# Retention attention feeding a gated MLP: tables on ScalarE's queue, the mask moved up, attention blocks set further apart

## The chip, the cores and the metric

The kernel runs on one core of one Trainium2 chip, in one launch. The metric is the device time of that launch in microseconds (us); the times shown are medians. The core's engines run side by side, each with its own list of instructions in a fixed order: TensorE (PE in the profile, its weight loads PEld), VectorE (DVE), ScalarE (ACT), GpSimd (POOL) and SyncE (SP), which only starts transfers here. They wait for each other by semaphores.

## The reference, cut to what matters

```python
# attention: batch 4, heads 8, seq 768, head_dim 64
gamma = 1.0 - 2.0 ** (-5.0 - np.arange(H))
for t in range(S):
    state = gamma * state + k_t v_t^T          # one 64x64 state per batch and head
    y[:, :, t] = (q_t @ state) / sqrt(D)
x = y.transpose(0, 2, 1, 3).reshape(B, S, H * D)   # 4 x 768 x 512
# MLP
gate = sigmoid(causal conv of x over time, 5 taps, per channel)
val = x @ w_val                                 # 512 x 512
out = (gate * val) @ w_out                      # 512 x 512
```

All inputs are float32; the weights and `conv_w` come as float64 words and are turned into float32 on the chip.

## The kernel before, in words

**Tiles.** The sequence is cut into 6 chunks of 128 tokens. An attention block `g` (0 to 23) is chunk `c = g // 4` of batch `b = g % 4`, all 8 heads. A chunk that is whole (4 blocks) gives `x` for the MLP: 4 `val` tiles (channels) and then 4 `out` tiles (batches), each of 12 matmuls of 128x512, because each product is made of three float32r matmuls (`xh`, `xl` are the rounded part of x and the rest; `wvh`, `wvl`, `woh`, `wol` those of the weights; `gvh`, `gvl` those of gate times val). 48 tiles in all; the last one is done in two halves.

**An attention block.** One 1 MB load `att` brings q, k, v, k (block 0 in two halves, q and k first); POOL scales v by a decay table (`decay`, L249). PE makes scores (`sy<-att`, L259). DVE masks them (`mask`, L269, writes `u`). Then PE does y from the masked scores (`y_scores`, `sy<-u,att`, L297) and the state update of the first half (`z_ps`, L281); both together are `block_a`. `block_b` is the second state update, y from the state that ACT copied (`snap`, L292), and from block 6 on the scores of the next block. DVE evacuates y into `x` (`evac`, L342). In PE's instructions each of the small products is a weight load and a matmul, done twice for float32: a block has 112 to 128 such pairs, a `val` or `out` tile 12.

**Beside it.** Each of the 8 weight pieces (512 KB, `wst`) is converted by five DVE steps, one of ACT and one of POOL (L386 to L415), and then split (L426, L430); `cw_raw`, the conv weights, takes the same path with 20 columns. For each `val` tile ACT does the first conv tap and DVE the other four (`tap`, L443; PE may take one or two instead), ACT the sigmoid, and DVE multiplies gate and val (`gated`, L478).

**What sets the order.** Every piece of work is a step, made by `at(due, engine, cost, reads, writes, ...)`. `plan` sorts the steps by `due`, and then walks through a modelled time: whenever an engine is free, it takes the ready step with the lowest `due`. The result is the fixed order of each engine's instructions. Costs and due times have no other effect. `LATE_STEP` spaces the due times of attention blocks 6 to 23 and `MLP_STEP` those of the tiles. In the model PE also waits for its instructions: after every `PAGE` pairs the next page is there `FETCH` us after the page before the last one ended.

**Transfers.** `get` loads the small tables: `small_sb` (decay, ratio and mask), `cw_raw`, `pos_sb`, `eye_sb`. All transfers start from SP, in the order of its list; each takes one of eight semaphores in turn, and the transfer that takes it again waits until the one before has landed. PE multiplies `pos_sb` into a base table (`first_pos`, L322) ahead of the first `y_scores`.

Of the kernel before, what the change touches and what calls it, by code (L numbers as in the profile page):

```python
# [27 lines left out]
LATENCY, LANDING = 0.15, 1.8  # L28
PAGE, FETCH = 128, 4.0
TINY = 2.0 ** -15 * (1.0 + 1.0 / 8.0)  # L30
# [10 lines left out]
class Step:  # L41
    def __init__(self, due, engine, cost, reads, writes, fn, args):
        self.due, self.engine, self.cost, self.fn, self.args = due, engine, cost, fn, args
        self.reads, self.writes = reads, writes
        self.waits, self.then = set(), []
        self.next = []
        self.after = []
        self.ready = 0.0
        self.words = 0
        self.other = None  # L50


def plan(steps):
# [39 lines left out]
    clock, free = {}, {}  # L93
# [11 lines left out]
    while any(free.values()):  # L105
# [11 lines left out]
        if e == "PE" and s.words:  # L117

            left, now = s.words, start
            while left >= words:  # L120
                now += s.cost * words / s.words
                left -= words
                paged.append(now)
                now, words = max(now, paged[-2] + FETCH), PAGE
            words -= left
# [7 lines left out]
        for t in s.then:  # L133
            late = LANDING if e == "DMA" else 0.0 if t.engine == e else LATENCY
            t.ready = max(t.ready, clock[e] + late)
            t.waits.discard(s.index)
# [7 lines left out]
def tile_retention_gated_mlp(  # L144
# [91 lines left out]
    def get(dst, src):  # L236
        nc.sync.dma_start(out=dst, in_=src)

# [293 lines left out]
    MM = 0.232  # L532
    EARLY_AT = 2.6
    EARLY_STEP = 2.8
    LATE_AT = 28.7
    LATE_STEP = 3.05
    MLP_AT = 31.2
    MLP_STEP = 10.2
    SPLIT_LEAD = 5.4
    CONV_LEAD = 6.1  # L540
    W_AT = (9.3, 15.6, 15.6, 22.7, 32.7, 35.7, 38.7, 41.7)

    loaded = {}

    def load_at(due, g):
        loaded[g] = due
        a = [("att", g % LB, "qk"), ("att", g % LB, "vk")]
        if g == 0:
            at(due, "DMA", 1.4, [], a[0:1], load, g, slice(0, 2))
            at(due, "DMA", 0.2, [], ["small"], get, small_sb, small)  # L550
            at(due, "DMA", 1.4, [], a[1:2], load, g, slice(2, 4))
            at(due, "DMA", 0.1, [], ["cwraw"], get, cw_raw,
               conv_w.bitcast(I32).rearrange("p (n two) -> p n two", two=2))
            at(due, "DMA", 0.1, [], ["pos"], get, pos_sb, pos)
        else:
            at(due, "DMA", 2.6, [], a, load, g)
# [11 lines left out]

    scored, summed = {}, {}

    def attention(g, t, ahead):
# [34 lines left out]
        if b == 0:  # L606
            xbufs[c] = Slot("x", XB)
            last = [xbufs[c - 1]] + [("x", c - 1, i) for i in range(B)] if c else []
            at(t + 3.5, "ACT" if c else "DVE", 0.25, last,
               [xbufs[c]] + [("x", c, i) for i in range(B)], new_x, c)  # L610
        at(t + 5.0, "DVE", 0.62, [y, ("dec", c % 2), xbufs[c]], [("x", c, b)], evac, g)
        if g + LB < NG:
# [82 lines left out]
    for i in range(WARM):  # L695
        at(0, "PE", 0.43, [], [Slot("acc", 2) if i < 2 else "sy1"], warm_up, i)
    at(0, "ACT", 1.5, [], ["table"], first_sigmoid)
    load_at(0, 0)
    for due, w, n in ((0.1, 1, 0), (0.2, 0, 1), (0.3, 1, 1), (0.4, 0, 2), (0.5, 1, 2), (0.6, 0, 3), (0.7, 1, 3), (0.8, 0, 4)):
        if w or n < LB:  # L700
            (load_w_at if w else load_at)(due, n)
        if due == 0.3:
            at(due, "DMA", 0.2, [], ["eye"], get, eye_sb, eye)
    at(5.05, "PE", 1.0, ["pos", ("att", 0, "vk")], ["sy1"], first_pos)
    at(5.06, "ACT", 0.6, ["sy1"], ["base", ("dec", 0)], base_copy)
    convert(4.0, "cw")
    for m in range(NPAIR):
# [117 lines left out]
```

## Time and profile before

| | |
|---|---|
| Median of 3 runs | 234.3 us (234.22 to 234.41) |
| Profiled execution, time | 235.24 us |
| Profiled execution, span from first to last instruction | 233.5 us |
| PE, DVE, ACT, POOL busy | 209.3, 140.2, 105.7, 105.7 us |
| Instructions of PE | 3549 weight loads, 3549 matmuls |

The profile comes from one execution, which was 0.9 us above the median; the time holds 1.7 us more than the span. Busy time of PE counts a matmul from its start to its modelled end, and matmuls overlap, so rate is read from the distance between starts.

### The profile page before, as it was taken

The page shows a single profiled execution, that of the slowest core. Times are in us where ns is not written, and L with a number is a line of the kernel's source. Part 1 is how long each engine was busy: PE and PEld are TensorE (multiplying, and loading weights), DVE is VectorE, ACT ScalarE, POOL GpSimd, SP SyncE. Part 2 cuts the span into 40 slices and gives each one's busy share as a digit, 9 for nine tenths or more (in the row PEclk, how much of TensorE's full clock was granted, in tenths as well). Part 3 has the DMA queues.
Part 4 walks back from the last instruction along what each step waited for, and adds up shares of the span by engine and source line. Part 5 has one row for each costly group of instructions (what it writes and reads, how often), then busy time and mean ns, then how long its engine had stood idle before and what let it go on. Part 6 is the DMA issues. An engine that isn't in the chain of part 4 may idle for free.

```text
span 233.5 us, 7952 instructions
## 1 busy us (share of the span) xinstructions
PE 209.3 (90%) x3549; PEld 163.5 (70%) x3549; DVE 140.2 (60%) x213; ACT 105.7 (45%) x218; POOL 105.7 (45%) x93
## 2 busy tenths in 40 slices
PE   8276666998799998897998999999999999999994
PEld 3166655766577776675776778888888888888884
DVE  0488678999999998322296636169617861921100
ACT  2363285238855842243544322664376426521322
POOL 0257879677996281116822020582078208220400
PEclk9975697999999999998899999999999999999999
DMA  5999979963565665545250101111111111111122
GB/s 155 381 428 413 380 276 345 414 234 117 181 219 206 243 239 199 206 173 215 65 213 3 48 4 49 45 46 45 48 45 45 45 47 63 59 58 45 45 93 90
DMA packets 8822, 36.32 MB, mean 156 GB/s; under 512 B 1106, under 2 KB 1618, under 8 KB 5844
## 3 DMA queue, kind: packets, MB, share of 16 engines
q1 hardware_dynamic: 8788, 35.82, 41.0%
q8 instruction: 28, 0.46, 0.8%
q14 instruction: 6, 0.05, 0.1%
HBM read 29.52 MB, written 6.29 MB: 153 GB/s over the span
## 4 chain that ended last, share of the span: by engine, by line
PE 61%; DVE 19%; issue 7%; POOL 5%; ACT 3%; DMA 3%; SPq 0%; POOLq 0%; ACTq 0%; DVEq 0%
PE mm L497 27%; PE mm L469 22%; DVE acc L443 9%; PE sy L297 6%; PE sy L259 3%; DMA att<-in_att_dram 3%; PE z_ps L281 3%; DVE x L342 3%; DVE u L269 2%; POOL rest L411 2%; POOL att L249 2%; DVE gate L478 1%; ACT xh L351 1%; DVE rest L415 1%; POOL wvl L430 1%
## 5 line engine op out<-in xcount | busy, mean ns | idle before, releaser
L443 DVE SCALAR_TENSOR_TENSOR acc<-x,cw_sb,acc 128x512 f32<-128x512 f32 x95 | 70.5, 753 | 17.2 <-ACT acc L441 15.1
L489 POOL TENSOR_TENSOR gvl<-gate,gvh 128x512 fp32r<-128x512 f32 x24 | 30.8, 1291 | 44.6 <-ACT gvh L485 34.4
L355 POOL TENSOR_TENSOR xl<-x,xh 128x512 fp32r<-128x512 f32 x24 | 30.5, 1284 | 31.8 <-PE mm L469 28.5
L497 PE MATMUL mm<-woh,gvh 128*128 128x512 f32 (+1 forms) x100 | 39.4, 394 | 0.0
L497 PE MATMUL mm<-wol,gvh 128*128 128x512 f32 (+1 forms) x100 | 39.3, 393 | 0.0
L497 PE MATMUL mm<-woh,gvl 128*128 128x512 f32 (+1 forms) x100 | 39.3, 393 | 0.0
L249 POOL TENSOR_TENSOR att<-att,small_sb 128x512 f32<-128x512 f32 x24 | 25.1, 1044 | 29.1 <-DMA att<-in_att_dram 27.3
L507 ACT COPY o_sb<-mm 128x512 f32<-128x512 f32 (+1 forms) x25 | 14.3, 571 | 37.0 <-PE mm L497 36.9
L269 DVE TENSOR_TENSOR u<-sy,small_sb 128x512 f32<-128x512 f32 x24 | 16.5, 686 | 24.0 <-PE sy L259 24.0
L478 DVE TENSOR_TENSOR gate<-mm,gate 128x512 f32<-128x512 f32 x24 | 16.4, 685 | 22.2 <-PE mm L469 22.2
L469 PE MATMUL mm<-xl,wvh 128*128 128x512 f32 x96 | 28.5, 407 | 0.0
L469 PE MATMUL mm<-xh,wvh 128*128 128x512 f32 x96 | 28.2, 410 | 0.0
L469 PE MATMUL mm<-xh,wvl 128*128 128x512 f32 x96 | 28.1, 404 | 0.0
L485 ACT CAST gvh<-gate 128x512 fp32r<-128x512 f32 x24 | 14.9, 620 | 26.2 <-DVE gate L478 17.6
L297 PEld LDWEIGHTS sy<-u,att 64*64 64x64 f32 x768 | 16.0, 152 | 14.4 <-issue 5.8
L259 PE MATMUL sy<-att 64*64 64x64 f32 x768 | 18.8, 232 | 7.4 <-issue 6.3
L297 PE MATMUL sy<-u,att 64*64 64x64 f32 x768 | 19.1, 243 | 5.9 <-DVE x L342 3.6
L281 PE MATMUL z_ps<-att 64*64 64x64 f32 x704 | 22.1, 240 | 2.3 <-issue 1.0
L292 ACT COPY snap<-z_ps 128x256 f32<-128x256 f32 x44 | 14.5, 371 | 19.0 <-PE z_ps L281 19.0
L281 PEld LDWEIGHTS z_ps<-att 64*64 64x64 f32 x704 | 17.3, 150 | 8.1 <-ACT snap L292 5.2
L259 PEld LDWEIGHTS sy<-att 64*64 64x64 f32 x768 | 15.9, 147 | 9.0 <-issue 7.0
L497 PEld LDWEIGHTS mm<-woh,gvh 128*128 128x128 f32 x100 | 18.9, 189 | 4.2
(46 smaller groups left out, 264.6 us busy)
## 6 DMA issues: line engine op xcount, KB each, us to landing
att<-in_att_dram SPq DMA_DIRECT2D x23, 1024.0 KB, 5.8
out_dram<-o_sb SPq DMA_DIRECT2D x23, 256.0 KB, 2.0
wst<-in_w_dram SPq DMA_DIRECT2D x8, 512.0 KB, 7.2
att<-in_att_dram SPq DMA_DIRECT2D x2, 512.0 KB, 5.5
out_dram<-o_sb SPq DMA_DIRECT2D x2, 128.0 KB, 1.7
small_sb<-in_small_dram SPq DMA_DIRECT2D x1, 68.0 KB, 4.1
eye_sb<-in_eye_dram SPq DMA_DIRECT2D x1, 64.0 KB, 8.5
cw_raw<-in_conv_w_dram SPq DMA_DIRECT2D x1, 20.0 KB, 6.4
```

Source lines behind the costliest of these rows:

```text
L249: nc.gpsimd.tensor_tensor(v, v, vd_sb[:, c, :].unsqueeze(2).broadcast_to([P, 8, HALF]), op=ALU.mult)
L259: nc.tensor.matmul(sy[cols, x, (2 * j + s) * HALF:(2 * j + s + 1) * HALF], lhsT=kT[rows, x, j, s, :], rhs=q[rows, x, j, s, :], start=True, ...
L269: nc.vector.tensor_tensor(us[g], sy[:, :, 0:256].rearrange("p x (a t) -> p x a t", t=HALF), tri_sb.unsqueeze(1).unsqueeze(1).broadcast_to( ...
L281: nc.tensor.matmul(z_ps[cols, x, b, j], lhsT=k[rows, x, j, s, :], rhs=v[rows, x, j, s, :], start=g == 0 and s == 0 and j == 0, stop=True, ...
L297: nc.tensor.matmul(sy_of(g)[cols, h, off:off + HALF], lhsT=lhsT, rhs=rhs, start=start, stop=True, skip_group_check=True,)
L355: nc.gpsimd.tensor_tensor(xl[n, ct], xs[n][:, ct, :, HALO:], xh[n, ct].bitcast(F32), op=ALU.subtract)
L443: nc.vector.scalar_tensor_tensor(acc, x[:, :, k:k + P], cw_sb[:, m, k:k + 1], acc, op0=ALU.mult, op1=ALU.add,)
L469: nc.tensor.matmul(vps[n, m], lhsT=w[:, m, ct * P:(ct + 1) * P], rhs=xx[n, ct].rearrange("p b t -> p (b t)"), start=(i == 0), stop=(i == 3 ...
L478: nc.vector.tensor_tensor(gv, vps.pop((n, m)), gv, op=ALU.mult)
L485: nc.scalar.copy(gvs[n, m][0], gate[n, m])
L489: nc.gpsimd.tensor_tensor(gvl, gate.pop((n, m)), gvh.bitcast(F32), op=ALU.subtract)
L497: nc.tensor.matmul(ops[n, b, cs.start][:, 0:cs.stop - cs.start], lhsT=gg[:, b * P:(b + 1) * P], rhs=w[:, ct, cs], start=(i == 0), stop=(i ...
```

## The change

Four things are changed. The small tables are loaded by ScalarE's queue, ahead of its table load, and no longer lie between SP's transfers; `first_pos` no longer waits for the second half of block 0. In the planner the page wait has two lengths (3.4 us, or 5.0 while transfers are under way, in place of 4.0). The costs and due times of the start are others: the conversion of `cw_raw` is due at 9.0 and not at 4.0. And due times are spaced otherwise: 6.0 for attention blocks in place of 3.05, 3.6 for tiles in place of 10.2, where a `val` tile is never due before its chunk is whole (`whole`). The work itself is the same.

```diff
-PAGE, FETCH = 128, 4.0
+PAGE, FETCH, CROWDED = 128, 3.4, 5.0
...
+        self.lag = 0.0
...
-                now, words = max(now, paged[-2] + FETCH), PAGE
+                slow = clock.get("DMA", 0.0) > now
+                now, words = max(now, paged[-2] + (CROWDED if slow else FETCH)), PAGE
...
-            t.ready = max(t.ready, clock[e] + late)
+            t.ready = max(t.ready, clock[e] + late + s.lag)
...
     def get(dst, src):
-        nc.sync.dma_start(out=dst, in_=src)
+        nc.scalar.dma_start(out=dst, in_=src)
...
-    LATE_STEP = 3.05
-    MLP_STEP = 10.2
+    LATE_STEP = 6.0
+    MLP_STEP = 3.6
...
         if g == 0:
-            at(due, "DMA", 1.4, [], a[0:1], load, g, slice(0, 2))
-            at(due, "DMA", 0.2, [], ["small"], get, small_sb, small)
-            at(due, "DMA", 1.4, [], a[1:2], load, g, slice(2, 4))
-            at(due, "DMA", 0.1, [], ["cwraw"], get, cw_raw,
+            at(due, "DMA", 3.2, [], a[0:1], load, g, slice(0, 2))
+            at(due, "DMA", 1.6, [], a[1:2], load, g, slice(2, 4))
+            at(due, "ACT", 0.4, [], ["small"], get, small_sb, small)
+            at(due, "ACT", 0.4, [], ["pos"], get, pos_sb, pos)
+            at(due, "ACT", 0.4, [], ["cwraw"], get, cw_raw,
                conv_w.bitcast(I32).rearrange("p (n two) -> p n two", two=2))
-            at(due, "DMA", 0.1, [], ["pos"], get, pos_sb, pos)
+            at(due, "ACT", 0.4, [], ["eye"], get, eye_sb, eye)
+            for s in steps[-4:]:
+                s.lag = 5.0
...
+        whole[c] = t + 5.1
...
-    at(0, "ACT", 1.5, [], ["table"], first_sigmoid)
     load_at(0, 0)
+    at(0.05, "ACT", 1.5, [], ["table"], first_sigmoid)
...
-        if due == 0.3:
-            at(due, "DMA", 0.2, [], ["eye"], get, eye_sb, eye)
-    at(5.05, "PE", 1.0, ["pos", ("att", 0, "vk")], ["sy1"], first_pos)
+    at(5.05, "PE", 1.0, ["pos"], ["sy1"], first_pos)
...
-    convert(4.0, "cw")
+    convert(9.0, "cw")
...
+    t = MLP_AT - MLP_STEP
     for p, (what, n, m) in enumerate(order):
-        t = MLP_AT + MLP_STEP * p
+        t += MLP_STEP
+        if what is val_tile:
+            t = max(t, whole[n] + max(SPLIT_LEAD, CONV_LEAD))
```

Lines from L44 on have numbers higher by one to seven in the changed file; the text below uses those of the kernel before, the rows of the changed order their own.

What this does to the order is shown at three places. First DVE, from its first instruction that waits for a transfer. `u<-sy,small_sb` is the mask of block 0, 128x20 are the conversion steps of `cw_raw`, `wst` is the first weight piece. Before:

```order
L386 TENSOR_SCALAR acc<-cw_raw 128x20
L392 SCALAR_TENSOR_TENSOR top<-cw_raw,acc 128x20
L398 TENSOR_SCALAR acc<-top 128x20
L402 SCALAR_TENSOR_TENSOR rest<-cw_raw,acc 128x20
L415 SCALAR_TENSOR_TENSOR cw_sb<-acc,rest 128x20
L386 TENSOR_SCALAR acc<-wst 128x512
L269 TENSOR_TENSOR u<-sy,small_sb 128x512
```

And now:

```order
L388 TENSOR_SCALAR acc<-cw_raw 128x20
L394 SCALAR_TENSOR_TENSOR top<-cw_raw,acc 128x20
L271 TENSOR_TENSOR u<-sy,small_sb 128x512
L400 TENSOR_SCALAR acc<-top 128x20
L404 SCALAR_TENSOR_TENSOR rest<-cw_raw,acc 128x20
L388 TENSOR_SCALAR acc<-wst 128x512
```

The mask has moved ahead of four instructions, but two short steps on `cw_raw` still stand before it.

Second DVE between the masks of blocks 6 and 7 (`x<-sy_97` and `x<-sy` are evacuations, `gate<-mm` is `gated`). Before, from the mask of block 6 to that of block 7:

```order
L269 TENSOR_TENSOR u<-sy,small_sb 128x512
L386 TENSOR_SCALAR acc<-wst 128x512
L342 TENSOR_TENSOR x<-sy_97,dec 128x4x128
L392 SCALAR_TENSOR_TENSOR top<-wst,acc 128x512
L398 TENSOR_SCALAR acc<-top 128x512
L402 SCALAR_TENSOR_TENSOR rest<-wst,acc 128x512
L443 SCALAR_TENSOR_TENSOR acc<-x,cw_sb,acc 128x512 x3
L269 TENSOR_TENSOR u<-sy,small_sb 128x512
```

Now, from the second instruction behind the mask of block 6 (two taps stand between):

```order
L344 TENSOR_TENSOR x<-sy_97,dec 128x4x128
L445 SCALAR_TENSOR_TENSOR acc<-x,cw_sb,acc 128x512
L388 TENSOR_SCALAR acc<-wst 128x512
L394 SCALAR_TENSOR_TENSOR top<-wst,acc 128x512
L400 TENSOR_SCALAR acc<-top 128x512
L404 SCALAR_TENSOR_TENSOR rest<-wst,acc 128x512
L445 SCALAR_TENSOR_TENSOR acc<-x,cw_sb,acc 128x512 x3
L417 SCALAR_TENSOR_TENSOR rest<-acc,rest 128x512
L445 SCALAR_TENSOR_TENSOR acc<-x,cw_sb,acc 128x512
L344 TENSOR_TENSOR x<-sy,dec 128x4x128
L480 TENSOR_TENSOR gate<-mm,gate 128x512
L271 TENSOR_TENSOR u<-sy,small_sb 128x512
```

Seven taps instead of three and one evacuation, one conversion step and one `gated` more stand ahead of the mask of block 7.

Third PE in the middle. Before, block 13 from its `y_scores` to the next block's scores and the first matmul behind them:

```order
L297 MATMUL sy<-u,att 64x64 x16
L281 MATMUL z_ps<-att 64x64 x8
L469 MATMUL mm<-xl,wvh 128x512 x3
L281 MATMUL z_ps<-att 64x64 x8
L297 MATMUL sy<-att,snap 64x64 x16
L259 MATMUL sy<-att 64x64 x16
L497 MATMUL mm<-woh,gvh 128x512
```

Now, block 17:

```order
L299 MATMUL sy<-u,att 64x64 x16
L283 MATMUL z_ps<-att 64x64 x8
L471 MATMUL mm<-xh,wvh 128x512 x4
L471 MATMUL mm<-xh,wvl 128x512 x4
L283 MATMUL z_ps<-att 64x64 x8
L299 MATMUL sy<-att,snap 64x64 x16
L261 MATMUL sy<-att 64x64 x16
L471 MATMUL mm<-xl,wvh 128x512 x4
```

Eight tile matmuls instead of three lie between the two halves of a block. Counted over the whole order, with the end of the attention in the last column:

| ahead of `y_scores` of block | 6 | 7 | 9 | 11 | 15 | 19 | 23 |
|---|---|---|---|---|---|---|---|
| tile matmuls on PE, before | 0 | 14 | 40 | 59 | 106 | 145 | 185 |
| tile matmuls on PE, now | 0 | 22 | 66 | 96 | 178 | 257 | 336 |
| taps / other 512-wide instructions on DVE up to the mask, before | 4/32 | 7/38 | 8/58 | 17/65 | 39/76 | 39/86 | 51/95 |
| the same, now | 4/32 | 11/41 | 15/62 | 27/69 | 46/80 | 55/91 | 70/103 |

In all there are 588 tile matmuls, the last 24 of half width. From the conversion of the first weight piece to the mask of block 15 DVE has 115 instructions before; from there to the mask of block 11 it has 96 now, one of them a short step on `cw_raw`. Weight loads and matmuls of PE up to the `y_scores` of block 11, 15 and 23 are 1484, 2043 and 3098 pairs before; now they are 1523, 2117 and 3251.

More of the change, by code (lines that the diff above doesn't have):

```diff
@@ L532, in tile_retention_gated_mlp @@
     MM = 0.232
-    EARLY_AT = 2.6
-    EARLY_STEP = 2.8
-    LATE_AT = 28.7
-    LATE_STEP = 3.05
-    MLP_AT = 31.2
-    MLP_STEP = 10.2
-    SPLIT_LEAD = 5.4
-    CONV_LEAD = 6.1
-    W_AT = (9.3, 15.6, 15.6, 22.7, 32.7, 35.7, 38.7, 41.7)
+    EARLY_AT = 3.46
+    EARLY_STEP = 2.26
+    LATE_AT = 29.71
+    LATE_STEP = 6.0
+    MLP_AT = 31.96
+    MLP_STEP = 3.6
+    SPLIT_LEAD = 5.44
+    CONV_LEAD = 6.16
+    W_AT = (9.3, 13.0, 15.6, 22.7, 36.8, 32.1, 37.6, 38.1)
     loaded = {}
@@ L567, in block_b @@
             scores(g + 1)
-    scored, summed = {}, {}
+    scored, summed, whole = {}, {}, {}
     def attention(g, t, ahead):
```

## The prediction

> **What bounds the kernel now.** I read the busy time by stage first, because the average over the span mixes stages with different limits. The columns are length, then busy us (and instructions) of PE, PEld, DVE, ACT and POOL, then the granted TensorE clock, the DMA share and GB/s:
>
> ```profile
> 0.00:9.92 9.92, 6.25 (x47) 2.44 (x47) 0.93 (x6) 1.88 (x4) 1.47 (x6) 1.00 0.76 245
> 9.92:40.33 30.41, 19.97 (x752) 17.92 (x752) 25.04 (x40) 17.03 (x42) 22.30 (x20) 0.74 0.95 375
> 40.33:92.72 52.39, 48.93 (x1214) 37.04 (x1213) 51.14 (x78) 29.98 (x65) 36.20 (x31) 0.99 0.62 225
> 92.72:140.70 47.98, 44.49 (x1143) 33.69 (x1144) 22.08 (x33) 18.24 (x42) 15.30 (x13) 0.96 0.33 118
> 140.70:230.40 89.70, 89.62 (x397) 72.45 (x395) 41.02 (x58) 38.17 (x66) 30.43 (x24) 1.00 0.14 54
> 230.40:233.50 3.10, 0.00 (x0) 0.00 (x0) 0.00 (x0) 0.37 (x1) 0.00 (x0) 0.86 0.19 68
> ```
>
> Nothing but tiles is left from 140.70 on: PE is full and can't be faster. From 40.33 to 92.72 DVE is busy 51.14 of 52.39 us, so DVE sets the pace. From 92.72 on it is idle for half of the time, and yet PE does not run at its rate. Before 40.33 neither is full. So there are three places to win: the start, DVE's stretch, and the stretch behind it.
>
> The timeline of the start shows why nothing moves until 11.31 (start, duration, engine, instruction, wait ahead of it):
>
> ```profile
> 0.74 0.37 SPq L234 DMA_DIRECT2D att<-in_att_dram  x1
> 1.17 0.42 SPq L237 DMA_DIRECT2D small_sb<-in_small_dram  x1
> 1.64 0.42 SPq L234 DMA_DIRECT2D att<-in_att_dram  x1
> 2.96 0.35 SPq L365 DMA_DIRECT2D wst<-in_w_dram  x1
> 5.21 0.69 PE L259 MATMUL sy<-att 64*64 64x64 f32 x32
> 8.38 1.12 PE L322 MATMUL sy<-pos_sb 2*128 2x512 f32 x2 [2.47 <-DMA pos_sb<-in_pos_dram]
> 8.43 1.04 POOL L249 TENSOR_TENSOR att<-att,small_sb 128x512 f32<-128x512 f32 x1 [7.99 <-DMA att<-in_att_dram]
> 8.62 0.18 DVE L386 TENSOR_SCALAR acc<-cw_raw 128x20 int32<-128x20 int32 x1 [7.69 <-DMA cw_raw<-in_conv_w_dram]
> 9.92 0.69 DVE L386 TENSOR_SCALAR acc<-wst 128x512 int32<-128x512 int32 x1
> 10.53 0.68 DVE L269 TENSOR_TENSOR u<-sy,small_sb 128x512 f32<-128x512 f32 x1
> 11.31 1.13 PE L297 MATMUL sy<-u,att 64*64 64x64 f32 x32 [1.81 <-issue]
> ```
>
> Scores are done at 5.90. The decay, which needs v, ends at 9.47; the mask, behind the steps on `cw_raw` and a weight piece, ends at 11.21. The mask is the later one.
>
> Then PE's own instructions. The page counts their loads, and the timeline shows PE stopping in the middle of a block with nothing to wait for:
>
> ```profile
> q8 instruction: 28, 0.46, 0.8%
> 18.41 0.80 PE L259 MATMUL sy<-att 64*64 64x64 f32 x18 [1.57 <-issue]
> 24.52 0.37 PE L259 MATMUL sy<-att 64*64 64x64 f32 x2 [2.05 <-issue]
> 96.69 0.34 PE L259 MATMUL sy<-att 64*64 64x64 f32 x7 [0.90 <-issue]
> 102.18 0.56 PE L259 MATMUL sy<-att 64*64 64x64 f32 x19 [0.26 <-issue]
> 108.93 0.68 PE L259 MATMUL sy<-att 64*64 64x64 f32 x29 [1.51 <-issue]
> PE sy L259 <- issue: 2.7, 3, 1.5
> ```
>
> 28 loads for 3549 pairs of weight load and matmul make 127 pairs a page. The stops lie 6.1 us apart at the start (18.41 to 24.52), and 5.5 and 6.75 us behind 92.72: so long does a page take when PE is through with the one before. The last row, the waits from 92.72 to 140, sums three of them.
>
> **The change, part by part.** I follow the path that ends last: DVE up to the last mask that PE waits for, and PE from there to the end. The rows for it:
>
> ```profile
> 75.44 3.78 DVE L443 SCALAR_TENSOR_TENSOR acc<-x,cw_sb,acc 128x512 f32<-128x512 f32 x5
> 79.13 0.68 DVE L269 TENSOR_TENSOR u<-sy,small_sb 128x512 f32<-128x512 f32 x1
> 79.73 0.68 DVE L342 TENSOR_TENSOR x<-sy,dec 128x512 f32<-128x512 f32 x1
> 91.29 0.68 DVE L269 TENSOR_TENSOR u<-sy,small_sb 128x512 f32<-128x512 f32 x1
> 92.72 0.69 PE L297 MATMUL sy<-u,att 64*64 64x64 f32 x32 [0.67 <-DVE x L342]
> 117.33 0.69 PE L297 MATMUL sy<-u,att 64*64 64x64 f32 x32
> 123.45 0.69 PE L297 MATMUL sy<-u,att 64*64 64x64 f32 x32
> 132.46 0.69 PE L297 MATMUL sy<-u,att 64*64 64x64 f32 x32
> 137.13 0.69 PE L297 MATMUL sy<-u,att 64*64 64x64 f32 x32
> 163.10 2.80 PE mm L469 x12
> 230.40 0.37 ACT o_sb L507
> ```
>
> Prices. DVE: five taps from 75.44 to 79.13 are 0.738 us each; from mask to evacuation, 0.60 for the others. PE: a tile is 2.80, a matmul of it 0.2333. From 117.33 to 123.45 (blocks 19 to 20) there are 15 tile matmuls, so a block takes 6.12 - 3.50 = 2.62; from 132.46 to 137.13 (22 to 23) there are 10, so in the last chunk, which has one state update less, 4.67 - 2.33 = 2.34.
>
> Where DVE hands over. Before, from mask 6 to mask 15, DVE has 35 taps and 44 others, 52.2 us by these prices; it let `y_scores` of block 15 start at 92.72. Now, from mask 6 to mask 11, it has 23 taps and 37 others, 39.2 us; PE has 96 tile matmuls and five blocks for it, 22.4 + 13.1 = 35.5. PE still waits. From mask 11 to mask 15 DVE has 19 and 11, 20.6 us, and PE 82 matmuls and four blocks, 29.6. So block 11 is the last that waits for DVE, and PE decides from there.
>
> *DVE's term.* From the first weight piece to that mask DVE has 96 instructions in place of 115: 12 taps and 8 others fewer, and one short step of 0.18 more. 12 x 0.738 + 8 x 0.60 - 0.18 = 13.5 us less, with the 5.4 and 1.3 us of idle time before and behind 40.33 (windows above) kept. The masks, evacuations and taps that now come later lie beside PE's work there.
>
> *The start.* SP has four issues fewer, of some 0.4 each. The second half of block 0 is issued at 1.17 and not 1.64, and the 68 KB of `small_sb` no longer lie ahead of it, which at this stage costs 0.35 us at 198 GB/s:
>
> ```profile
> 3.00:4.00 1.00, 1.00 (x4) 0.32 (x3) 0.00 (x0) 0.00 (x0) 0.00 (x0) 1.00 0.85 198
> ```
>
> It then lands at 7.6 and not 8.43, the decay ends at 8.65, and `y_scores` starts at 8.75: 2.55 earlier, if the mask is done. That needs `cw_raw` by 7.7, since two steps on it still stand first: issued third on ACT, at about 1.6, it may take 6.1 us. The first weight piece is issued about 1.3 earlier, so DVE's chain from 9.92 gains 0 to 1.3, and PE's pages, asked for as PE goes along, gain what `y_scores` gains. Between 1.3 and 2.55 I take 2.0. Bounds: 0.5 (the issue alone, 1.64 to 1.17) and 4.7 (the mask right behind the scores, 5.90 + 0.69, and v there in time). ACT's four issues, 1.7 us, and its table load end near 4; its next work needs `pos_sb`, so they are hidden by that wait, and if `pos_sb` came first, by PE's wait for v. `first_pos` no longer waits for v: it then lies beside the wait for the mask. The next weight piece on SP now waits for `small_sb`, but 1.5 MB are queued ahead of it.
>
> The Trainium skill speaks against this part: "DMA: Bandwidth & Descriptors", section "Issuing engines are not separate DMA queues", has transfers of all issuing engines interleave on the same 16 DMA engines, so that a second issuer saves the issue time only. By that rule the start would be worth 0.5.
>
> So `y_scores` of block 11 starts at 92.72 - 13.5 - 2.0 = 77.2.
>
> *PE's term.* Behind it lie 588 - 96 = 492 tile matmuls, 24 of half width: 480 x 0.2333 = 112.0. Blocks 11 to 19 are 9 x 2.62 = 23.6, blocks 20 to 23 4 x 2.34 = 9.4. Together 145.0.
>
> *Losses of PE.* The same count for before, from block 15: 470 x 0.2333 + 5 x 2.62 + 4 x 2.34 = 132.1, where 230.40 - 92.72 = 137.7 were used; 5.6 were lost in nine blocks, half of it (2.7) in stops for pages. There a page was used up in (132.1 less the tiles behind block 23, 93.5) / 8.2 pages = 4.7 us, less than the 5.5 to 6.75 it takes to come. Now from block 11 to 23 there are 13.5 pages, and for them 240 x 0.2333 + 9 x 2.62 + 3 x 2.34 = 86.6 us: 6.4 us a page. Nearest to the intervals shown, I let a third of the pages lose 0.35, 1.5 us in all. Bounds: 0, and the old loss for each of 13 blocks, 8.0.
>
> "Runtime: NRT & Kernel Launch" of the Trainium skill, section "Instruction fetch mechanics", calls the crossing of a 16 KiB boundary "mostly hidden". The rows above disagree: 0.26 to 2.05 us at such places, here where most instructions are short. By the rule the spacing would buy nothing and the old loss would stay.
>
> *What moves at no cost.* The loads of later blocks wait for buffers that come free later; POOL waits for transfers, as it does now, with the next decays done ahead. The last chunk's taps and gates come later: behind the mask of block 23 DVE has 24 taps and 9 others, 23 us, under 56 us of tiles. The tail from 230.40 is unchanged, 3.1.
>
> Sum: 77.2 + 145.0 + 1.5 + 3.1 = 226.8 of span against 233.5. The profiled time is 1.7 above the span and the median 0.9 below the profiled time, so the median is 227.6 against 234.3, 2.9% faster.
>
> **The rivals.** *The start saves its issue time only.* `small_sb` and `cw_raw` then share the DMA engines with the loads and v comes no sooner: 0.5 in place of 2.0, 228.3 of span, median 229.1. For it: at 3.00 to 4.00 the DMA share is already 0.85. Against: v lay behind `small_sb` in one queue.
>
> *Better.* v and `cw_raw` by 5.9, and no page stop: 226.8 - 2.7 - 1.5 = 222.6, median 223.4. For it: 68 KB and 20 KB took 4 to 6 us behind others only.
>
> *The spacing does not do what it is counted for.* Stops come per block and not per page in time: 8.0 in place of 1.5, 233.3, median 234.1, the same. Against: the stops lie a page apart.
>
> *Slower: pages come slower than they are used.* In the stretch from block 11 to 23 a page is allowed 6.4 us. If its loads, with transfers now spread through that stretch, took longer each time, the stretch would last 13.5 times that. From 7.1 us on (86.6 + 8.7, the gain without losses) nothing is left; at 7.4 it is 99.9, 13.3 more than 86.6: 238.6 of span, median 239.4. For it: 6.75 came at half DMA load, longer than 6.1 at full load, so load is not all that decides. Against: 6.75 is the longest shown here.
>
> **How the numbers follow.** The forecast 0.50; the start at its issue time 0.15; better 0.12; the spacing without effect 0.10; slower pages 0.13. The time is the forecast's, 227.6, whose own range is 225 to 230. The range reaches from 222.5 to 234.0: a third of the better case (0.04) lies below, the slower case (0.13) above, 0.17 in all. A difference under 0.2% can't be told from no change here. Faster: the first three and 0.04 of the fourth, 0.81; same 0.06; slower 0.13.
>
> **What the profile will show.** The first `y_scores` near 8.8; the first masks behind two steps on `cw_raw`; `y_scores` of block 11 near 77 with DVE full up to there; from there a distance of about 7.7 us between blocks (22 tile matmuls and 2.62); block 23 near 165; stops without a releaser of under 2 us behind 77; tiles alone for some 56 us at the end. I am wrong if `cw_raw` lands behind 7.7 and holds DVE, if PE waits for DVE still behind block 11, or if stops recur with every page.

## The result, and the profile after

The changed kernel takes 228.45 us (median of 4 runs, 227.65 to 229.25) against 234.36 us (4 runs, 234.22 to 235.38): a ratio of 0.974, 95% interval 0.969 to 0.978. On a second chip it was 228.41 us and 0.970 (0.965 to 0.976). The forecast was 227.6. The profiled execution took 227.65 us with a span of 225.9. The experiments ran on other chips than this first comparison; each ratio below is to the kernel before on the chip of that run. Times in us are medians of all executions, while the ratios leave out the few executions that took over 1.5% longer than the fastest of their kernel.

The stages of the changed kernel, in the columns of the first table of the prediction (length, busy us and instructions of PE, PEld, DVE, ACT, POOL, then granted clock, DMA share, GB/s):

```profile
9.92:40.33 30.41, 21.73 (x757) 19.16 (x758) 26.37 (x44) 16.17 (x41) 23.46 (x21) 0.72 0.94 371
40.33:78.59 38.26, 35.05 (x689) 26.35 (x688) 37.40 (x57) 23.07 (x46) 28.87 (x24) 1.00 0.51 185
78.59:171.90 93.31, 93.31 (x1833) 72.75 (x1832) 56.84 (x84) 45.26 (x95) 37.95 (x32) 1.00 0.37 127
222.80:225.90 3.10, 0.00 (x0) 0.00 (x0) 0.00 (x0) 0.37 (x1) 0.00 (x0) 0.90 0.24 85
```

DVE's full stretch now ends at 78.59, not at 92.72, and behind it PE is busy for all of the 93.31 us at a clock of 1.00, where before it was 44.49 of 47.98 at 0.96. The third stage of before, PE neither full nor waiting for DVE, is gone. The stage ahead of 40.33 is much as it was, at a clock of 0.72 (0.74 before).

The timeline of the changed kernel's start, and where block 11 takes over (start, duration, engine, instruction, wait):

```profile
1.74 0.35 ACTq L239 DMA_DIRECT2D cw_raw<-in_conv_w_dram  x1
7.18 1.04 POOL L251 TENSOR_TENSOR att<-att,small_sb 128x512 f32<-128x512 f32 x1 [6.74 <-DMA att<-in_att_dram]
9.15 0.18 DVE L388 TENSOR_SCALAR acc<-cw_raw 128x20 int32<-128x20 int32 x1 [8.22 <-DMA cw_raw<-in_conv_w_dram]
9.46 0.68 DVE L271 TENSOR_TENSOR u<-sy,small_sb 128x512 f32<-128x512 f32 x1
10.24 1.13 PE L299 MATMUL sy<-u,att 64*64 64x64 f32 x32 [3.38 <-DVE acc L400]
10.36 0.69 DVE L388 TENSOR_SCALAR acc<-wst 128x512 int32<-128x512 int32 x1
17.11 0.71 PE L261 MATMUL sy<-att 64*64 64x64 f32 x17 [0.41 <-issue]
23.28 0.21 PE L261 MATMUL sy<-att 64*64 64x64 f32 x1 [2.36 <-issue]
28.30 0.36 PE L283 MATMUL z_ps<-att 64*64 64x64 f32 x1 [0.64 <-issue]
38.21 0.52 PE L299 MATMUL sy<-att,snap 64*64 64x64 f32 x20 [1.39 <-issue]
77.27 0.68 DVE L271 TENSOR_TENSOR u<-sy,small_sb 128x512 f32<-128x512 f32 x1
78.59 0.69 PE L299 MATMUL sy<-u,att 64*64 64x64 f32 x32
86.29 0.69 PE L299 MATMUL sy<-u,att 64*64 64x64 f32 x32
164.76 0.69 PE L299 MATMUL sy<-u,att 64*64 64x64 f32 x32
```

v is there at 7.18, 1.25 earlier than before. But `cw_raw`, issued at 1.74 on ScalarE's queue, lands only at 9.1, and the two steps on it hold DVE and the mask behind them. The first `y_scores` starts at 10.24 (11.31 before), the first weight step at 10.36, which is 0.44 *later* than before. Then come the stops for pages, and at 38.21 PE stands at the same place and goes on at the same time as before. From block 11 to 23 PE goes 86.17 us without a wait. The stop in the kernel before:

```profile
38.21 0.81 PE L297 MATMUL sy<-att,snap 64*64 64x64 f32 x20 [1.37 <-issue]
```

**Where the 7.6 us of span came from.** I take the prices of the prediction for PE (0.2333 a tile matmul, 2.62 or 2.34 a block) and one conv tap on PE, 1.08, and subtract them from the time between two `y_scores`. What is left is PE's loss:

| stretch | before | now |
|---|---|---|
| start of `y_scores` of block 6 | 38.71 | 38.51 |
| from block 6 to 23 | 98.42, work 87.9 | 126.25, work 123.2 |
| PE's loss there | 10.5 | 3.1 |
| of it up to the handover (block 15; 11) | 4.6 | 3.5 |
| of it behind the handover | 5.9 | -0.4 |

So 7.4 of the 7.6 us are idle or slow time of PE behind block 6 that is gone, most of it behind the handover, and 0.2 is the start. For each undisturbed block the work priced so came out within 0.06 us of the time measured, mostly a little high; twelve blocks of that make the -0.4.

### The profile page after: what moved, and what is told of

Same layout as the page of the kernel before. It is cut to its first block, busy times and chain, and to the rows that moved or that the text cites. A ratio compares the mean times of both kernels' runs of the same rounds, so it can differ in the third digit from the quotient of the medians.

```text
span 225.9 us, 7949 instructions
## 1 busy us (share of the span) xinstructions
PE 206.9 (92%) x3551; PEld 161.9 (72%) x3551; DVE 140.3 (62%) x212; ACT 105.9 (47%) x218; POOL 105.9 (47%) x93
## 4 chain that ended last, share of the span: by engine, by line
PE 80%; DVE 9%; issue 4%; DMA 3%; ACT 1%; POOL 1%; ACTq 0%; POOLq 0%; DVEq 0%
PE mm L499 31%; PE mm L471 27%; PE sy L299 11%; PE z_ps L283 5%; PE sy L261 5%; DMA cw_raw<-in_conv_w_dram 3%; DVE acc L445 2%; DVE u L271 1%; DVE x L344 1%; DVE acc L400 1%; PE acc L454 1%; DVE top L394 1%; DVE acc L388 1%; DVE rest L404 1%; DVE rest L417 1%
## 5 line engine op out<-in xcount | busy, mean ns | idle before, releaser
L471 PE MATMUL mm<-xl,wvh 128*128 128x512 f32 x96 | 27.8, 403 | 0.0
L471 PE MATMUL mm<-xh,wvl 128*128 128x512 f32 x96 | 27.4, 400 | 0.0
L344 DVE TENSOR_TENSOR x<-sy,dec 128x512 f32<-128x512 f32 x20 | 13.8, 688 | 14.0 <-PE sy L261 13.8
L461 ACT ACTIVATE gate<-acc 128x512 f32<-128x512 f32 x24 | 14.3, 598 | 17.1 <-POOL gvl L491 10.1
L294 ACT COPY snap<-z_ps 128x256 f32<-128x256 f32 x44 | 15.2, 373 | 14.8 <-PE z_ps L283 14.3
L499 PEld LDWEIGHTS mm<-wol,gvh 128*128 128x128 f32 x100 | 18.8, 188 | 4.1
L499 PEld LDWEIGHTS mm<-woh,gvl 128*128 128x128 f32 x100 | 18.8, 188 | 4.1
```

Source lines behind the costliest of these rows:

```text
L294: nc.scalar.copy(sn, z_ps[:, :, b])
L344: nc.vector.tensor_tensor(xs[c][:, :, b, HALO:].rearrange("p (h j) t -> p h j t", h=2), sy_of(g)[:, :, 256:512].rearrange("p h (j t) -> p ...
L471: nc.tensor.matmul(vps[n, m], lhsT=w[:, m, ct * P:(ct + 1) * P], rhs=xx[n, ct].rearrange("p b t -> p (b t)"), start=(i == 0), stop=(i == 3 ...
L499: nc.tensor.matmul(ops[n, b, cs.start][:, 0:cs.stop - cs.start], lhsT=gg[:, b * P:(b + 1) * P], rhs=w[:, ct, cs], start=(i == 0), stop=(i ...
```

## Experiments

I asked three things: which part of the change carries the gain, what sets the moment of the handover, and what became of the lead at the start.

**The tables alone.** The kernel before with its tables on ScalarE's queue.

```diff
-            at(due, "DMA", 0.2, [], ["small"], get, small_sb, small)
...
+            at(due, "ACT", 0.4, [], ["small"], get, small_sb, small)
...
-        nc.sync.dma_start(out=dst, in_=src)
+        nc.scalar.dma_start(out=dst, in_=src)
```

> The kernel before with the tables alone moved to ScalarE's queue; spacing, page waits and the due time of the conversion stay. Theory A (the spacing carries the gain, and the start's lead is taken back by block 6): first y_scores near 10.3 as in the changed kernel, y_scores of block 6 within 0.6 us of before's 38.7, time 233.7 to 234.5. Theory B (the lead of the first y_scores, 1.07 us, is carried to the end): 233.3. Theory C (the tables are what made the kernel faster): below 230.

Ratio 0.999 (0.995 to 1.002), 235.4 us: no effect that can be told from none. The timeline:

```profile
8.27 0.18 DVE L387 TENSOR_SCALAR acc<-cw_raw 128x20 int32<-128x20 int32 x1 [7.33 <-DMA cw_raw<-in_conv_w_dram]
9.36 0.92 PE L298 MATMUL sy<-u,att 64*64 64x64 f32 x24 [1.79 <-issue]
37.60 0.59 PE L298 MATMUL sy<-u,att 64*64 64x64 f32 x25 [0.48 <-DVE u L270]
43.97 1.01 PE L260 MATMUL sy<-att 64*64 64x64 f32 x25 [3.09 <-issue]
```

Here 1.1 us of a lead of 1.95 were still there at block 6 (37.60 against 38.71), which is theory B's. Then a page came 7.4 us after the one before it (PE had stopped for that until 36.55), and a stop of 3.09 us took the lead. But this execution took 237.6 us, 2.2 more than the median, so it can't tell what the others lost there, and theory B's 233.3 us, a ratio of 0.995, lies at the edge of the interval: between A and B the run does not decide. Theory C is out.

**The spacing alone.** The kernel before with the four edits of spacing and nothing else.

```diff
-    LATE_STEP = 3.05
-    MLP_STEP = 10.2
+    LATE_STEP = 6.0
+    MLP_STEP = 3.6
...
+            t = max(t, whole[n] + max(SPLIT_LEAD, CONV_LEAD))
```

> The kernel before with the spacing alone: due times 6.0 apart for attention blocks, 3.6 for tiles. DVE has 30 taps and 68 others up to the mask of block 11, the changed kernel 27 and 68. Theory A (spacing carries the gain; DVE's count up to block 11 sets the handover): first y_scores at 11.3, y_scores of block 11 at 78.6 + 3 x 0.738 + 0.2 = 81.0, no waits without a releaser behind it, time 228.5 + 2.4 = 230.9. Theory B (the start's 1.07 us is carried as well): 231.7. Theory C (the tables made it faster): 234 or more.

Ratio 0.986 (0.981 to 0.990), 232.0 us. `y_scores` of block 11:

```profile
82.39 0.69 PE L297 MATMUL sy<-u,att 64*64 64x64 f32 x32
```

That is 1.4 later than counted; the largest wait ahead of it is one of 4.09 us, from 56.56 on, in which PE stands for ScalarE's first tap of a tile. The span of 229.6 is this plus 147.2. Half of the whole gain is here. Of the 3.0 to 3.8 us between this block 11 and the changed kernel's, the three taps more make 2.2.

**One page wait.** The changed kernel with one length of page wait in the planner.

```diff
-PAGE, FETCH, CROWDED = 128, 3.4, 5.0
+PAGE, FETCH, CROWDED = 128, 4.0, 4.0
```

> The changed kernel with the planner's page wait back at one length, 4.0 us. DVE has 29 taps and 68 others up to the mask of block 11 instead of 27 and 68; PE's order behind block 11 has the same count of tiles per block. Theory A (DVE's count sets the handover): y_scores of block 11 at 78.6 + 1.5 = 80.1, time 229.9. Rival (DVE has slack enough by then, two taps are swallowed): 228.5.

Ratio 0.983 (0.978 to 0.989), 231.6 us; `y_scores` of block 11 at 81.99, span 229.3. Block 6 came early, at 36.21, but two taps more (1.5) and a new wait of DVE, 3.38 us for a weight piece at 42.15, turned that round. The two lengths matter through the order that comes out.

**The mask first.** The changed kernel with a later `cw_raw` in the planner, so that the mask of block 0 is DVE's first.

```diff
-                s.lag = 5.0
+                s.lag = 8.0 if s.fn is get and s.args[0] is cw_raw else 5.0
```

> The changed kernel with cw_raw taken as 3 us later in the planner: DVE now starts with the mask of block 0, and the steps on cw_raw stand behind it. First y_scores near 8.9 instead of 10.24 in both theories. DVE has 28 taps up to the mask of block 11 instead of 27. Theory A (a lead at the start is taken back by block 6): y_scores of block 6 within 0.4 us of 38.5, time 228.4 to 229.2. Theory B (carried): y_scores of block 6 at 37.2, time 227.2 to 227.9.

Ratio 0.980 (0.975 to 0.985), 230.6 us: not faster than the changed kernel, though the start is as early as could be asked for:

```profile
6.82 0.69 DVE L271 TENSOR_TENSOR u<-sy,small_sb 128x512 f32<-128x512 f32 x1 [5.89 <-PE sy L261]
7.96 0.69 PE L299 MATMUL sy<-u,att 64*64 64x64 f32 x32
...
38.06 0.56 PE L299 MATMUL sy<-att,snap 64*64 64x64 f32 x20 [2.04 <-issue]
```

A lead of 2.28 us at the first `y_scores` is one of 0.15 at the page that came by 38.06 (38.21 in the changed kernel; 38.74 in its second trace, below). That is theory A's, but neither had the rest: this order puts three tile matmuls on PE and four taps more on DVE ahead of block 6, which came at 40.70, and block 11 at 80.44.

**The changed kernel again**, for comparison on one chip with the next three.

> The changed kernel once more, on the chip that the next three runs use, to compare them with. In all spaced kernels so far the span is y_scores of block 11 plus 147.2 or 147.3. Expected: ratio to before 0.972 to 0.978, and the span again y_scores of block 11 plus 147.3.

Ratio 0.970 (0.965 to 0.976), 228.4 us. Block 6 at 39.24, block 11 at 79.44, span 226.7: again 147.3 behind block 11. `cw_raw` landed 0.6 us earlier here than in the first trace, at 8.4, and the first weight step started at 9.74, 0.18 earlier than in the kernel before. Yet block 6 came later: in this execution the stops from 17 to 45 us add up to 6.1 and not 4.8:

```profile
9.74 0.69 DVE L388 TENSOR_SCALAR acc<-wst 128x512 int32<-128x512 int32 x1
22.32 0.26 PE L261 MATMUL sy<-att 64*64 64x64 f32 x1 [2.20 <-issue]
28.23 0.27 PE L283 MATMUL z_ps<-att 64*64 64x64 f32 x1 [1.53 <-issue]
38.74 0.81 PE L299 MATMUL sy<-att,snap 64*64 64x64 f32 x20 [2.38 <-issue]
```

**Wider spacing.** Attention blocks due 7.5 apart.

```diff
-    LATE_STEP = 6.0
+    LATE_STEP = 7.5
```

> The changed kernel with attention blocks due 7.5 apart instead of 6.0: 118 tile matmuls on PE and 30 taps and 68 others on DVE ahead of block 11, instead of 96, 27 and 68. Theory A (DVE's count sets the handover and PE runs without loss behind it): y_scores of block 11 at 78.6 + 3 x 0.738 = 80.8, behind it 147.3 - 22 x 0.2333 = 142.2, span 223.0, 1.3% less than the changed kernel. Rival (the further tiles make PE wait for converted weights and gates, or PE becomes the bound up to block 11: 118 x 0.2333 + 13.1 = 40.6 from block 6 and the losses of 4.6): y_scores of block 11 at 83.7 or later, span 225.9, no gain.

Ratio 0.979 (0.974 to 0.984), 230.5 us: slower than 6.0, and the rival was right and too mild. `y_scores` of block 11 came at 85.68, though its mask was done at 82.2: PE, with 22 tile matmuls more ahead of it, was late by itself by then. Behind it lie 143.3 us, where 142.2 were counted. The mask:

```profile
81.56 0.68 DVE L271 TENSOR_TENSOR u<-sy,small_sb 128x512 f32<-128x512 f32 x1
```

**A quarter of the loads.** From block 5 on only v is loaded, over the tiles of five blocks earlier.

```diff
+        if g >= LB:
+            tiles[g], part = tiles[g - LB], slice(2, 3)
-        if part.start == 0:
+        elif part.start == 0:
```

> The changed kernel, but from block 5 on only v is loaded, 256 KB instead of 1 MB, and the other three parts stay those of five blocks earlier (this leaves work out); the order of PE and DVE is the same. In the changed kernel PE stands still for its instructions at pairs 222, 349, 477 and 730, 4.8 us in all from 17 to 45. Theory P (a page of instructions comes late because it shares the DMA engines with data): the stops fall below 2.5 us, y_scores of block 6 comes at 37.0 or earlier. Rival L (a page takes 5 to 6 us whatever else is moved): stops of 4 to 6 us, y_scores of block 6 at 38 to 38.5, time within 0.5 us of the changed kernel.

Ratio 0.964 (0.959 to 0.970), 227.3 us, 1.1 less than the changed kernel on that chip. Of the stops only the first is left, which falls where the first five blocks and the weights still come in. The timeline, with `y_scores` of blocks 6 and 11, and the window from 10 to 40:

```profile
22.10 0.21 PE L263 MATMUL sy<-att 64*64 64x64 f32 x1 [2.05 <-issue]
37.36 0.65 PE L301 MATMUL sy<-u,att 64*64 64x64 f32 x32
77.90 0.69 PE L301 MATMUL sy<-u,att 64*64 64x64 f32 x32
```

```profile
10.00:40.00 30.00, 21.83 (x759) 19.29 (x758) 26.18 (x42) 16.67 (x41) 24.54 (x22) 0.68 0.69 259
```

The DMA share from 10 to 40 is 0.69 instead of 0.94, the stops are 2.05 us instead of 6.1, and block 6 comes 1.9 us earlier than in the comparison, block 11 1.5. PE and DVE have the same order as in the changed kernel, so this shows theory P: pages are late because data are under way.

**Eight taps less.** The last two taps of chunk 0's four conv tiles are left out.

```diff
-            step.fn(*step.args)
+            if not (step.fn is tap and step.args[0] == 0 and step.args[2] > 2):
+                step.fn(*step.args)
```

> The changed kernel without the last two taps of the four conv tiles of chunk 0: 8 DVE instructions less, all ahead of the mask of block 11 (this leaves work out); everything else in the same order. Theory A (DVE's count up to block 11 sets the time): 8 x 0.738 = 5.9 us less on DVE, until PE's own 35.5 us from block 6 to 11 bounds it, so y_scores of block 11 at 74.0 to 76.8 and the span 1.8 to 4.6 us shorter than the changed kernel's. Rival (PE's stops and the start set it): less than 0.5 us.

Ratio 0.963 (0.957 to 0.968), 226.4 us, 2.0 less than the changed kernel on that chip; the profiled execution is the fastest of six. Its `y_scores` of block 11, and the window ahead of it:

```profile
75.98 0.69 PE L299 MATMUL sy<-u,att 64*64 64x64 f32 x32
```

```profile
40.33:75.98 35.65, 34.55 (x686) 26.29 (x685) 33.48 (x51) 20.99 (x42) 28.82 (x24) 1.00 0.50 188
```

The span is 223.3, 3.4 less than the comparison's 226.7, and block 11 is earlier by the same 3.5; by the medians, 2.0, the gain is at the lower end of theory A's 1.8 to 4.6. DVE is no longer full (33.48 of 35.65) and PE nearly is. So it is DVE's count up to the mask of block 11 that sets the end, until PE's own work does.

**Narrower spacing.** Attention blocks due 4.5 apart.

```diff
-    LATE_STEP = 6.0
+    LATE_STEP = 4.5
```

> The changed kernel with attention blocks due 4.5 apart instead of 6.0: 84 tile matmuls on PE and 28 taps and 67 others on DVE ahead of block 11, instead of 96, 27 and 68; from block 11 to 23 PE uses 12.9 pages in 169 x 0.2333 + 9 x 2.62 + 3 x 2.34 = 70.0 us, 5.4 us a page instead of 6.4 (4.7 in the kernel before). Theory A (only the tiles behind the handover count): y_scores of block 11 within 1 us of 79.5, behind it 147.3 + 12 x 0.2333 = 150.1, span 229.5, no waits without a releaser behind it. Rival P (pages come slower than 5.4 us with data under way, as in the kernel before, and stop PE again): the same y_scores of block 11, but 1 to 3 us of waits without a releaser from there to block 23, span 230.5 to 232.5.

Ratio 1.011 (1.005 to 1.017): slower than the kernel before, and both theories were too mild. The median of all six executions is 240.9 us, but three of them took 242 to 245; the profiled one took 238.4. Block 11 came at 80.43 and 156.2 us lay behind it, 6.1 more than the 150.1 counted. One page stop, from 89.65 on, and what followed it:

```profile
89.65:91.50 1.85, 0.00 (x0) 0.00 (x0) 0.79 (x2) 0.44 (x1) 1.85 (x2) 1.00 0.45 133
92.95:96.36 3.41, 3.41 (x50) 2.46 (x51) 2.32 (x5) 0.00 (x0) 1.24 (x2) 0.50 0.15 55
96.36:99.77 3.41, 3.41 (x103) 2.72 (x98) 2.28 (x4) 0.65 (x2) 0.00 (x0) 1.00 0.25 36
```

The stop lasts 1.85 us, and from 1.45 us after it the clock is 0.50 for 3.41 us: 1.7 us more. Two masks (1.2) and a wait for ScalarE's `snap` (0.7) make 5.5 of the 6.1. Ahead of block 11 DVE has one tap more than at 6.0, and PE, with 12 tile matmuls less, only waited more. From block 6 to 23 PE's loss, counted as above, is 12.7 us; it was 10.5 in the kernel before and 3.1 in the changed one.

**The start in another order.** The changed kernel with other due times ahead of block 6 and other page waits in the planner (1.6 and 4.9 us), meant as a better version.

```diff
-PAGE, FETCH, CROWDED = 128, 3.4, 5.0
+PAGE, FETCH, CROWDED = 128, 1.6, 4.9
...
-    EARLY_AT = 3.46
-    EARLY_STEP = 2.26
+    EARLY_AT = 4.11
+    EARLY_STEP = 4.15
...
-    W_AT = (9.3, 13.0, 15.6, 22.7, 36.8, 32.1, 37.6, 38.1)
+    W_AT = (10.6, 19.9, 18.8, 19.0, 38.6, 32.2, 38.9, 40.2)
...
```

> The changed kernel with other due times at the start: the mask of block 0 ahead of cw_raw, early blocks 4.15 apart instead of 2.26, weight conversions due at 10.6, 18.8, 19.0, 19.9, 32.2, 38.6, 38.9 and 40.2, so that DVE converts where it waited for PE. 26 taps and 68 others ahead of the mask of block 11 (27 and 68 before that), 97 tile matmuls on PE instead of 96. Theory A (the time is the mask of block 11: DVE's work up to it and DVE's waits ahead of it): waits of DVE from 9 to 80 fall from 3.5 to 5.3 us to below 3, y_scores of block 11 at 76 to 77, span 223.1 to 224.3. Rival (the page stops at pairs 349, 477 and 730 hold PE and with it DVE as before): y_scores of block 11 at 78.6 to 79.4, span 225.9 to 226.7.

Ratio 0.970 (0.965 to 0.975), 229.6 us (226.6 to 230.6): not better than the changed kernel, only less even. Block 11 at 81.03 in a profiled execution of 229.9 us; the waits of DVE did not shrink but changed (total, times, longest):

```profile
DVE acc L388 <- DMA wst<-in_w_dram: 2.9, 1, 2.9
DVE x L344 <- PE sy L261: 2.0, 1, 2.0
DVE acc L445 <- PE acc L454: 1.6, 1, 1.6
```

**Stops made on purpose.** To see whether a stop costs more than its length, masks are done several times over, so that PE waits for them in the stretch where it ran without a stop.

```diff
+        for _ in range({13: 5, 15: 5, 17: 5, 19: 5, 21: 8}.get(g, 1)):
```

> The changed kernel with the masks of blocks 13, 15, 17 and 19 done five times and that of block 21 eight times over (work added, the result stays). In the changed kernel these masks are done 1.9, 1.55, 0.8, 0.4 and 2.0 us ahead of y_scores and PE runs there without a stop at a clock of 1.00, so PE should now stand still for about 0.5, 0.9, 1.6, 2.0 and 2.2 us, 7.2 in all. Theory H (PE's clock falls to 0.50 for about 3.5 us after some stops, as at 108.93 in the kernel before, and each time costs 1.7 us beside the stop): half clock behind one or more of the three longest, none behind the two shortest; the span is longer by the stops and 1.7 for each, 9 to 12 us. Rival (a stop costs its own length alone; the lower clock in the kernel before came from something else, such as the transfers): clock 1.00 behind all of them, span 7.2 longer.

Ratio 1.027 (1.019 to 1.035), 240.7 us (238.8 to 243.9). The profiled execution is the fastest of the four, span 237.0. Its waits of PE from 90 to 170 us (total, times, longest), and windows at and around the last and longest stop:

```profile
PE sy L300 <- DVE u L272: 10.2, 5, 3.0
```

```profile
159.33:162.37 3.04, 0.00 (x1) 0.00 (x1) 2.90 (x6) 0.00 (x0) 0.00 (x0) 1.00 0.18 71
157.38:160.79 3.41, 1.95 (x9) 1.24 (x7) 3.27 (x5) 0.91 (x2) 0.00 (x0) 1.00 0.20 79
160.79:164.20 3.41, 1.83 (x52) 1.46 (x52) 3.27 (x6) 0.65 (x2) 0.00 (x0) 1.00 0.00 0
164.20:167.62 3.42, 3.42 (x74) 2.83 (x74) 2.90 (x5) 0.00 (x0) 0.00 (x0) 1.00 0.02 5
```

The stops came out longer than planned, 10.2 us in all, and the stretch behind block 11 is 157.8 instead of 147.3: 10.5 longer. The clock stayed at 1.00 even behind 3.04 us. So in this execution theory H fell: length alone does not bring the half clock.

What decides, in these traces, is how long PE stands still within one window. In each trace the clock changes only at moments that are a whole number of 3.41 us apart, and these moments fall at other places of the program in each execution. The windows of 3.41 us above are cut at them: the stop of 3.04 us is shared by two windows, and PE is busy for 1.95 and 1.83 us of them. (From 1.6 to 1.85 us both outcomes occur; the last section counts them.) The stop of 1.85 us in the run with narrower spacing lies in one window, with PE busy for 1.55; half a clock follows:

```profile
89.54:92.95 3.41, 1.55 (x13) 1.18 (x7) 2.04 (x4) 0.55 (x1) 3.32 (x3) 1.00 0.69 262
```

Two runs show it with the same work on PE. In the kernel before, and with the tables alone moved, PE stops at the same place of its program, with the same instructions around it, for 1.51 and 1.48 us. In the first the stop lies in one window and the clock is 0.50 in the next; in the second it is shared by two windows and the clock stays at 1.00. The window of the first, then the stop and the first of the two windows of the second:

```profile
106.31:109.72 3.41, 1.83 (x82) 1.61 (x82) 0.06 (x1) 0.56 (x2) 3.41 (x3) 1.00 0.34 82
111.68 0.68 PE L260 MATMUL sy<-att 64*64 64x64 f32 x28 [1.48 <-issue]
107.58:110.99 3.41, 2.54 (x98) 1.85 (x87) 0.00 (x0) 2.04 (x5) 2.00 (x2) 1.00 0.39 159
```

The three other executions were 2 to 5 us longer, two of them at a mean clock of 0.93 to 0.94 instead of 0.96, so the half clock may have come there.

**The tables back on SP.** The changed kernel with the first part undone.

```diff
-            at(due, "ACT", 0.4, [], ["small"], get, small_sb, small)
...
+            at(due, "DMA", 0.2, [], ["small"], get, small_sb, small)
...
-        nc.scalar.dma_start(out=dst, in_=src)
+        nc.sync.dma_start(out=dst, in_=src)
```

> The changed kernel with the tables back on SP's queue in the places that they had before, and first_pos waiting for v again; spacing, page waits and the other due times stay. The conversion of cw_raw stands ahead of the first mask again, and DVE has 28 taps and 68 others ahead of the mask of block 11 instead of 27 and 68, PE four of its own taps instead of two. Theory A (the tables buy nothing beyond a little issue time, since page stops take a lead back by block 6): first y_scores near 11, y_scores of block 6 at 38 to 39.3 as in the changed kernel, y_scores of block 11 within 1.5 us of 79, time 0 to 1.5 us above the changed kernel's 228.4. Rival (the lead of 1 to 1.7 us at the first y_scores is carried on): y_scores of block 6 at 39.5 to 41, time 230 to 232.

Ratio 0.981 (0.976 to 0.987), 230.6 us, 2.2 more than the changed kernel. First `y_scores` at 10.37, 0.13 and 0.75 later than in the two traces of the changed kernel; block 6 at 39.50 (38.51 and 39.24 there), block 11 at 81.30:

```profile
7.53 1.04 POOL L251 TENSOR_TENSOR att<-att,small_sb 128x512 f32<-128x512 f32 x1 [7.09 <-DMA att<-in_att_dram]
7.68 0.18 DVE L388 TENSOR_SCALAR acc<-cw_raw 128x20 int32<-128x20 int32 x1 [6.75 <-DMA cw_raw<-in_conv_w_dram]
10.37 0.92 PE L299 MATMUL sy<-u,att 64*64 64x64 f32 x24 [1.44 <-issue]
```

The time is the rival's, the way to it is not: 0.3 to 1.0 us come from ahead of block 6, and from block 6 to 11 it takes 41.8 instead of 40.1 or 40.2: in this order PE does two conv taps more there (2.16), and DVE one more (0.74). On SP's queue `cw_raw` landed at 7.6 here and at 8.1 and 8.5 in the two other kernels that load it there, v at 7.4 to 8.3; on ScalarE's queue, in eleven traces, `cw_raw` landed at 8.2 to 9.1 and v at 6.4 to 7.0. By the medians the move brought v 1.3 us forward and held `cw_raw`, on which the mask waits too, back by 0.3. So the queue itself brought little, and the planner's other order for it fits the rest.

**What the runs say together.** `y_scores` of block 11, and what lies behind it up to the end of the span:

| kernel | block 6 | block 11 | span | behind 11 |
|---|---|---|---|---|
| changed | 38.51 | 78.59 | 225.9 | 147.3 |
| changed, again | 39.24 | 79.44 | 226.7 | 147.3 |
| spacing alone | 38.48 | 82.39 | 229.6 | 147.2 |
| one page wait | 36.21 | 81.99 | 229.3 | 147.3 |
| mask first | 40.70 | 80.44 | 227.7 | 147.3 |
| quarter loads | 37.36 | 77.90 | 225.2 | 147.3 |
| eight taps less | 37.87 | 75.98 | 223.3 | 147.3 |
| tables back | 39.50 | 81.30 | 228.6 | 147.3 |
| start in another order | 40.64 | 81.03 | 228.0 | 147.0 |

With the same spacing the stretch behind block 11 is the same to 0.1 us (the last row has one tile matmul less behind it, 0.23), and all that differs is when block 11 starts. Block 6 hardly tells it: with one page wait it came at 36.21, and block 11 at 81.99.

The parts do not add up. The spacing alone brings 1.4%, the tables alone nothing that can be told, and the whole 2.6 to 3.0%; without the tables' move it is 1.9%, with one page wait 1.7%. So about half of the gain is the spacing's own, and the rest comes only with the order that all parts together give ahead of block 11. The other costs and due times of the start were not tried alone.

## Why the prediction was right, and where its sizes were off

The path was the one that the prediction described: DVE up to block 11, PE alone behind it. That its sum was only 0.9 us off in span is partly luck: the handover came 1.4 us later than forecast, and PE behind it took 2.3 us less.

- *Start, 2.0.* This is the term that failed. It assumed `cw_raw` by 7.7; it came at 9.1, held DVE, and the first weight step was 0.44 later instead of up to 1.3 earlier. In the second trace it was 0.18 earlier, and in none of the eleven traces with the tables on ScalarE's queue did `cw_raw` land ahead of 8.17. At block 6, 0.2 were left of the lead, and in the second trace nothing. The fault lies a step deeper: I took the lead of `y_scores` as carried on by PE's pages, "asked for as PE goes along". The mask-first run gave the full lead and lost all but 0.15 of it by 38.06, and with fewer loads under way all stops but one vanished. A lead ahead of a stretch in which instructions come late with the data is spent there. The price of the issue alone, 0.5, was the nearer bound. By "DMA: Bandwidth & Descriptors" of the Trainium skill, section "Issuing engines are not separate DMA queues", a second issuer saves issue time only. The time of the kernel agrees (tables alone 0.999, 0.995 to 1.002); the landing of v does not quite, which was issued 0.47 earlier and came 1.3 earlier by the medians above.
- *DVE's term, 13.5.* From the first weight step to the deciding mask it was 81.37 (9.92 to 91.29) and is 66.91 (10.36 to 77.27): 14.5 less, and 13.0 less in the second trace (9.74 to 78.12). Right to 1.0 us, and the run without eight taps shows that it is this count that decides.
- *PE's term, 145.0, and losses, 1.5.* From 78.59 PE took 144.2 to its last matmul, with no loss at all. 6.4 us a page was enough everywhere behind block 11; I had let a third of the pages be late.
- *Handover.* Predicted at 77.2; 78.59: the start costs 2.4, DVE's term gives back 1.0. *Steps of 7.7 us between blocks:* 6.8 to 7.7. *Block 23 near 165:* 164.76. *Tail, 3.1:* 3.10.
- *The profiled execution against the median.* I carried over that it lies 0.9 above the median; this time it lies 0.8 below. That is 1.7 more, the span is 0.9 less: 228.45 and not 227.6. This shift is chance.

Of the rivals, "start at its issue time" (229.1) was the nearer on the start, and its time is nearer than the forecast's (0.65 against 0.85 us). "The spacing does not do what it is counted for" and "pages come slower" are out: at this spacing no traced execution stopped for a page behind block 11. The old loss of 5.6 was more than stops for pages: the stop of 1.51 ahead of 108.93 in the kernel before was followed by half a clock,

```profile
110.00:113.20 3.20, 3.20 (x53) 2.35 (x51) 1.55 (x3) 0.62 (x1) 2.26 (x2) 0.51 0.51 210
```

another 1.7 us, which the prediction had not seen. "Runtime: NRT & Kernel Launch" of the Trainium skill, section "Instruction fetch mechanics", calls the crossing to the next block of instructions mostly hidden. At this rate of short matmuls and with data under way the runs disagree, with stops of 0.2 to 3.1 us; they agree once PE needs a page only every 6.4 us.

## What to carry to other kernels

Find the instruction at which the engine that paces the first half hands over to the one that paces the second, and price the work of the first engine ahead of that point and of the second behind it; in this kernel, leads won ahead of that point moved the end by less than their own size. A lead won at the very start is worth something only if nothing takes it back before that point: here it was the pages of instructions, which come late while data are under way. When due times space the work, there is a middle to be found: 4.5 was slower than the kernel before, 6.0 the best of the three tried, and 7.5 gave a third of the gain back.

## What the runs showed of the hardware

- PE's stops for instructions lie at the same places in its program whatever the kernel: ahead of pairs 222, 349, 477, 603, 730 and 858 of weight load and matmul (to within one or two, since some records are missing), 127 or 128 apart. The distance in time between two such stops in a row was mostly 3.7 to 6.8 us ahead of 45 us, and 7.4 to 8.1 us in three cases; with a quarter of the loads all but one were gone.
- PE's granted clock changed, in all 14 traces, only at moments a whole number of 3.41 us apart. I cut the traces into windows there, from 8 us on to 4 us from the end. A window at full clock in which PE was busy for under 1.6 us was followed by half clock in 25 of 25 cases, one with over 1.85 us in none of 755, and one in between in 4 of 9. A window at half clock in which PE is busy throughout costs 1.7 us. Ahead of block 6 every kernel had some. "TensorE: Matmul & The Clock Gate" of the Trainium skill, section "Part 1: The HAM clock gate (the "warmup" mystery)", has the clock halved after an idle window of about 3.4 us in a free-running raster. The raster and its length agree; that the window has to be wholly idle does not, since a stop of 1.85 us was enough.
- A 20 KB table of short rows landed 6.4 to 7.3 us after its issue on ScalarE's queue behind two others (eleven traces), and 5.5 to 6.4 us after its issue on SP's (three traces).
